# Batch 0 of a linear-attention and mixture-of-experts kernel rearranged: split loads of v, gate weights by GpSimd's queue, copies on either engine, a new written-out order

## The chip, the cores and the metric

The kernel runs on one core of one Trainium2 chip. A core has TensorE (matrix products and transposes, results in PSUM), VectorE and ScalarE (element-wise work; both read PSUM), GpSimd (here it fills constants and issues the loads of the expert weights), SyncE (issues most loads and stores) and 16 DMA engines that move data between the chip's memory (HBM) and the on-core memory (SBUF). Every engine takes its instructions in the order in which the program gives them. They run beside each other and meet at semaphores.

The metric is the device time of one execution in microseconds (us). A trace of one further execution says what each engine did and when.

## The reference, cut to what matters

```python
# q, k, v: batch 8, heads 8, sequence 576, head size 64
phi = lambda x: np.where(x > 0, x, np.exp(x) - 1.0) + 1.0
kv  = einsum('bhsd,bhse->bhde', phi(k), v);  z = phi(k).sum(axis=2)
x   = einsum('bhsd,bhde->bhse', phi(q), kv) / (einsum('bhsd,bhd->bhs', phi(q), z) + 1e-6)
# x as 8 batches of 576 rows of 512; 8 experts, hidden size 1024
logits = x @ w_gate                     # 512 x 8
local  = sigmoid(x @ w_local)           # 512 x 1
# along the rows of a batch: e = argmax(logits) where local < 0.5 or at row 0,
#                            else the expert of the row before
out[b, s] = softmax(logits[b, s])[e] * (relu(x[b, s] @ w1[e]) @ w2[e])
```

So the attention of a batch comes first, then a choice of expert for each row, then two matrix products with that expert's weights.

## The kernel before, in words

The kernel bets that all rows of a batch go to one expert, the one of its row 0. It computes each batch with that expert and counts the rows for which the bet failed; at the end a branch runs `general`, a slow and complete version, if the count is not zero. With these inputs it is zero.

A batch has two groups of four heads, so there are 16 groups, n = 0 to 15; batch a has groups 2a and 2a + 1. One group of q, k or v is 576 KB. All the work is cut into named steps, and `ORDER` (lines 23 to 71) writes out in which order they are issued. That text fixes the order on each engine, and `name/3` says which of four PSUM slots (two banks each) the step uses. The steps:

- `Lk.n`, `Lq.n`, `Lv.n`: loads of a group, by SyncE's queue. k has four buffers, q two, v three; a load waits until the buffer's last reader is done, and everything behind it on SyncE waits as well. Batch 0's q is loaded without its first of nine column blocks; that block comes on its own, in 64 KB pieces, by ScalarE's and by GpSimd's queue (`load_q0`).
- `E0`, `P0`: phi of that first block. `E.x.n`: exp, on ScalarE. `E2.x.n`: relu in place, on ScalarE. `P.x.n`: phi put together on VectorE, min(exp, 1) + relu. For k of batch 0 the relu is replaced by a clamp on VectorE, `CL.n` = max(x + 1, 1), and `P.k` takes the minimum.
- `VC.n`: v copied beside a column of ones. `K.n`: 72 matmuls for kv and z in one, `KC.n` its copy out of PSUM.
- `QL.a`, `Q.n`: transposes of phi(q) on TensorE (last 64 rows; the other 512), `QLC`, `QC` their copies on ScalarE.
- `NL.a`, `N.a.j.h`: numerator and denominator for the last rows, and for half h of group j; `DL`, `D`: the divisions on VectorE. `XL`, `X`: transposes of the result x, with the copies `XLC`, `XC`. `R.a.0`, `R.a.1`: logits of the last rows (row 0 is among them) and of the others, `RC` the copies.
- `PK.a`: the index of row 0's expert. `W.a.0`, `W.a.1`: GpSimd reads the index and issues the loads of w1 and w2, cast from float32 to bfloat16. Three slots keep the experts of earlier batches; a batch whose expert is there loads nothing. `CW`: the copy from slot to working buffer (for batch 0 the other way), on VectorE.
- `H.a.m`: one of eight hidden blocks, `HC` its relu out of PSUM, on ScalarE. `O0.a`, `O.a.i`: output blocks, `OC` the scaled copy, on ScalarE. `ST`: the stores. `S1`, `S2`, `S3`: the softmax factor.
- `HOLD`: a tiny SyncE transfer out of w1's last column, so that the loads behind it wait until batch 0's w1 is there.

Batches overlap: while batch a is in its hidden and output steps, the attention steps of batch a + 1 and the loads for a + 2 run in between. Before batch 0's first useful matmul TensorE runs filler matmuls on zeros (line 705).

Of the kernel before, what the change touches and what calls it, by code (L numbers as in the profile page):

```python
# [951 lines left out]
```

## Time and profile before

| | us |
|---|---|
| three runs, median | 222.1 (222.0 to 224.09) |
| the profiled execution, its own time | 222.04 |
| its span (first to last instruction) | 219.9 |
| busy: TensorE matmuls | 205.6 (94%) |
| busy: ScalarE | 153.3 (70%) |
| busy: VectorE | 151.7 (69%) |
| busy: GpSimd | 12.3 (6%) |

Busy time of TensorE includes the filler matmuls at the start. The rows that the text below shows are of three kinds. A window row gives a stretch of the span, its length, and the busy time of each engine in it, with the number of its instructions. A timeline row gives start, duration, engine, source line, operation, `out<-in` by the program's names, shapes, `xN` for N merged instructions and, in brackets, how long the engine had stood idle and what ended that. A DMA row gives the size and the time from issue to landing. PE is TensorE, PEld its weight loads, DVE VectorE, ACT ScalarE, POOL GpSimd, SPq and ACTq the queues of SyncE and ScalarE.

### The profile page before, as it was taken

To read this page: it belongs to the slowest core of one execution; us is meant where nothing else is said; L and a number is where in the kernel's file an instruction comes from. 1 tells how busy PE (TensorE), PEld (TensorE's weight loads), DVE (VectorE), ACT (ScalarE), POOL (GpSimd) and SP (SyncE) were. 2 spreads that over 40 slices of the span, in tenths; PEclk is the share of its full clock that TensorE was granted. 3 is DMA by queue.
4 is the path that set the end of the run, shared out by engine and by line. 5 is a ranking of instruction groups with operands and counts; after the bars stand their busy time and mean duration, and the time that the engine had idled before them with its cause. 6 is when DMAs were issued, how large, how long until landed. Compare 5 with 4: busy or idle time off the path is not lost.

```text
span 219.9 us, 8513 instructions
## 1 busy us (share of the span) xinstructions
PE 205.6 (94%) x3686; PEld 149.2 (68%) x3701; DVE 151.7 (69%) x428; ACT 153.3 (70%) x226; POOL 12.3 (6%) x41
## 2 busy tenths in 40 slices
PE   7777699999999999999999999999999999999990
PEld 2366578568876877865888668875888577657650
DVE  0687892999889899995795947967957659334000
ACT  3887968798988898899479647898544255327640
POOL 4005000000000011010000000110000001100000
PEclk9999999999999999999999999999999999999998
DMA  5999999387699568999299365999470025990083
GB/s 187 386 345 369 197 215 397 131 286 262 221 271 364 177 266 262 220 212 228 82 298 402 121 218 132 395 189 199 133 289 3 3 101 130 182 189 2 7 332 104
DMA packets 24141, 46.77 MB, mean 213 GB/s; under 512 B 2834, under 2 KB 8978, under 8 KB 23202
## 3 DMA queue, kind: packets, MB, share of 16 engines
q1 hardware_dynamic: 16834, 37.51, 48.2%
q0 software_dynamic: 6832, 8.45, 23.5%
q8 instruction: 31, 0.51, 0.9%
q10 hardware_dynamic: 432, 0.20, 0.4%
q14 instruction: 12, 0.10, 0.1%
HBM read 61.88 MB, written 9.44 MB: 324 GB/s over the span
## 4 chain that ended last, share of the span: by engine, by line
PE 87%; DMA 4%; ACT 3%; issue 1%; DVE 1%; SPq 1%
PE hps L532 29%; PE yps L551 25%; PE nps L349 8%; PE kvps L297 7%; PE tq L308 6%; DMA qraw<-in_q_dram 4%; PE yps L555 4%; PE tx L383 3%; PE lps L416 1%; SPq L138 1%; ACT qT L314 1%; DVE xb L337 1%; PE tql L322 1%; PE npl L368 1%; PE lps L410 1%
## 5 line engine op out<-in xcount | busy, mean ns | idle before, releaser
L532 PE MATMUL hps<-xT,w1cur 128*128 128x288 bf16 x512 | 66.9, 286 | 0.4 <-issue 0.3
L551 PE MATMUL yps<-w2cur,hT 128*128 128x512 bf16 x241 | 58.4, 379 | 0.8
L539 ACT ACTIVATE hT<-hps 128x576 bf16<-128x576 f32 x64 | 41.5, 655 | 24.8 <-PE hps L532 24.7
L532 PEld LDWEIGHTS <-w1cur 128*128 128x128 bf16 x512 | 48.7, 98 | 13.2 <-issue 0.8
L551 PEld LDWEIGHTS <-hT 128*128 128x128 bf16 x256 | 24.1, 98 | 25.5 <-ACT hT L539 0.2
L565 ACT ACTIVATE yo<-yps,pr 128x512 f32<-128x512 f32 x32 | 21.3, 686 | 12.9 <-PE yps L551 10.0
L276 DVE SCALAR_TENSOR_TENSOR fq<-fq,qraw 128x576 f32<-128x576 f32 (+1 forms) x32 | 22.5, 742 | 2.5 <-ACT qraw L247 2.4
L337 DVE TENSOR_TENSOR xb<-nps,rec 128x512 bf16<-128x512 f32 x32 | 22.1, 692 | 1.1
L349 PE MATMUL nps<-kv,qT 64*64 64x65 f32 x1024 | 21.0, 222 | 1.5 <-ACT qT L314 1.0
L297 PE MATMUL kvps<-vone,kraw 64*64 64x65 f32 x1152 | 20.0, 220 | 1.6 <-ACT qT L328 0.8
L314 ACT COPY qT<-tq 128x512 f32<-128x512 f32 x32 | 18.3, 641 | 4.4 <-PE tq L308 4.4
L349 PEld LDWEIGHTS nps<-kv,qT 64*64 64x64 f32 x1024 | 17.5, 134 | 5.4 <-issue 2.4
L297 PEld LDWEIGHTS kvps<-vone,kraw 64*64 64x64 f32 x1152 | 18.2, 134 | 3.5 <-ACT qT L328 1.0
L241 ACT ACTIVATE ek<-kraw 128x1152 f32<-128x1152 f32 x16 | 18.5, 1160 | 2.6 <-DMA kraw<-in_k_dram 2.2
L241 ACT ACTIVATE fq<-qraw 128x1152 f32<-128x1152 f32 (+1 forms) x16 | 18.5, 1156 | 0.7 <-DMA qraw<-in_q_dram 0.7
L269 DVE SCALAR_TENSOR_TENSOR kraw<-ek,kraw 128x1152 f32<-128x1152 f32 x14 | 18.8, 1348 | 0.3 <-ACT kraw L247 0.3
L247 ACT ACTIVATE qraw<-qraw 128x1152 f32<-128x1152 f32 (+1 forms) x16 | 18.3, 1148 | 0.1
L308 PE MATMUL tq<-ident,fq 128*128 128x128 f32 x128 | 16.4, 274 | 0.0
L247 ACT ACTIVATE kraw<-kraw 128x1152 f32<-128x1152 f32 x14 | 16.3, 1166 | 0.0
L308 PEld LDWEIGHTS tq<-ident,fq 128*128 128x128 f32 x128 | 14.3, 141 | 0.5
L388 DVE COPY xT<-tx 128x1024 bf16<-128x1024 bf16 x16 | 10.8, 683 | 3.5 <-PE tx L383 3.5
L288 DVE COPY vone<-vraw 128x1152 f32<-128x1152 f32 x15 | 11.7, 784 | 0.0
(93 smaller groups left out, 176.4 us busy)
## 6 DMA issues: line engine op xcount, KB each, us to landing
kraw<-in_k_dram SPq DMA_DIRECT2D x16, 576.0 KB, 4.9
vraw<-in_v_dram SPq DMA_DIRECT2D x16, 576.0 KB, 6.7
qraw<-in_q_dram SPq DMA_DIRECT2D x14, 576.0 KB, 5.8
w1s<-in_moe_w_dram POOLq DMA_DIRECT2D x7, 1024.0 KB, 10.3
w2s<-in_moe_w_dram POOLq DMA_DIRECT2D x7, 1024.0 KB, 11.5
out_dram<-yo SPq DMA_DIRECT2D x14, 512.0 KB, 5.0
qraw<-in_q_dram SPq DMA_DIRECT2D x2, 512.0 KB, 8.2
w1cur<-in_moe_w_dram POOLq DMA_DIRECT2D x2, 512.0 KB, 7.4
```

The source lines that it names most:

```text
L241: nc.scalar.activation(e[:, :, c0:c1, :], raw_, Act.Exp)
L247: nc.scalar.activation(raw_, raw_, Act.Relu)
L276: nc.vector.scalar_tensor_tensor(e[:, g], e[:, g], 1.0, r[:, g], Alu.min, Alu.add)
L297: nc.tensor.matmul(ps[g * PH:(g + 1) * PH, t, :W], lhsT=f[h, g, c, :], rhs=vo[h, g, c, :], start=(c == 0), stop=(c == C - 1))
L308: nc.tensor.transpose(ps[:, r, i * P:(i + 1) * P], ex_[n, "q"][:, 1 + i + (NC - 1) * r, :, :], identity=ident)
L314: nc.scalar.copy(qT[n][:, :, :SM].rearrange("q t (i p r) -> q r t i p", i=NC - 1, r=2)[:, r], ps[:, r, :].rearrange("q (i t p) -> q t i p" ...
L337: nc.vector.tensor_tensor(dst, ps[:, :, :, :Dh].rearrange("p g (i t) e -> p g i t e", t=2), rec.rearrange("p g (i t o) -> p g i t o", t=2, ...
L349: nc.tensor.matmul(ps[o * PH:(o + 1) * PH, g, (il * 2 + t) * W:(il * 2 + t + 1) * W], lhsT=qT[n][g * PH:(g + 1) * PH, t, i * P + o * PH:i ...
L532: nc.tensor.matmul(ps[:, u, :HS], lhsT=w1b[:, kk, m * P:(m + 1) * P], rhs=xT[b][:, kk, u * HS:(u + 1) * HS], start=(kk == 0), stop=(kk == ...
L539: nc.scalar.activation(hT[b][:, m, :].rearrange("p (u s) -> p u s", u=2), open_.pop(("H", b, m))[:, :, :HS], Act.Relu)
L551: nc.tensor.matmul(ps, lhsT=hT[b][:, m, i * P:(i + 1) * P], rhs=w2b[:, m, :], start=(m == 0), stop=(m == FK - 1))
L565: nc.scalar.activation(ym[:, i, :], ps, Act.Copy, scale=pr[:, i:i + 1])
```

## The change

Eight things change together.

1. v of groups 0 and 1 is loaded, copied beside its ones and used in two pieces, of five and of four column blocks (`Lv.n`, `Lv.n.1`; the same for `VC` and `K`).
2. `CL.1` writes into k's third buffer instead of in place (`CL.0` keeps v's third buffer).
3. The gate weights (w_gate, w_local) come by GpSimd's queue at the very start, as four rows of 4 KB and four of 512 B in k's fourth buffer. Nine TensorE transposes (`WT`) and a copy on VectorE (`WG`) turn them into the layout needed. Before, SyncE loaded them in rows of 32 and 4 bytes. The iota and its cast on GpSimd go.
4. The first column block of batch 0's q is one load by ScalarE's queue.
5. w1 of batch 0 comes in three pieces (first quarter, second quarter, second half) instead of two halves. There are two `HOLD`s now: one on the second quarter, one, much later in the order, on the end.
6. Batch 0's expert index is taken straight from PSUM, ahead of the copy of the logits.
7. Copies may run on either engine: a `^` behind a step in `ORDER` puts it on the engine other than its usual one. 23 of 64 `HC`, 20 of 40 `OC`, 14 `E2` and 2 `QC` so move from ScalarE to VectorE; 11 `VC` (three of them pieces of batch 0), 9 `XC`, 8 `KC` and 5 `XLC` are on ScalarE.
8. The filler is nine small matmuls and 15 large ones ahead of `WT`, instead of 19 large ones ahead of `QL.0`. `ORDER` is new as a whole, with new PSUM slots. The steps of the branch at the end (`FR`) stand at other places.

```diff
@@ ORDER (the first words; the old ones are in the listing above)
+Lq.0 Lk.1 FILL/0 Lv.1 Lv.1.1 Lv.0 Lk.0 Lq.1 Lv.0.1 E0.0 P0.0 E.k.1 CL.1 WT/1 E.q.0 P.k.1 QL.0/2 VC.1^
+E2.q.0^ QLC.0 K.1/3 VC.1.1^ P.q.0.0 K.1.1 E.k.0 P.q.0 CL.0 Q.0/2 Lq.2 VC.0^ Lk.3 P.k.0 E.q.1 Lk.2 KC.1^
+VC.0.1 QC.0 K.0/3 E2.q.1^ K.0.1 P.q.1.0 KC.0^ P.q.1 E.q.2 NL.0/2 N.0.0.1/3 DL.0 Lq.3 E.k.3 Lv.3 WG D.0.0.1
+XL.0/2 Lv.2 Q.1/1 XLC.0^ R.0.0/2 QC.1 N.0.0.0/3 RC.0.0 D.0.0.0 W.0.0 E.k.2 N.0.1.1/2 N.0.1.0/1 PK.0 E2.k.3
+D.0.1.1 E.q.3 D.0.1.0 BK.0 P.k.3 VC.3^ W.0.1 X.0.0/3 X.0.1/2 XC.0.0 XC.0.1^ K.3/1 E2.q.2^ E2.q.3^ R.0.1/3
+HOLD.0 H.0.0/2 P.q.3 Lk.5 H.0.1/0 HC.0.0 P.q.2 H.0.2/2 HC.0.1 H.0.3/0 KC.3 RC.0.1 S1.0 QL.1/1 CW.0.0 Q.3/3
+QLC.1 HC.0.2 H.0.4/1 E2.k.2 HC.0.3^ H.0.5/2 QC.3 P.k.2 Q.2/0 HC.0.4^ H.0.6/3 QC.2 VC.2 N.1.1.1/1 HC.0.5 Lv.5
...
-    fills = {("QL", 0): 19}
+    fills = {("WT",): 15}
...
-        def load_q0(n):
-            load(q0[:, n], q, n, 0, 1, nc.scalar if n else nc.gpsimd)
+        def load_q0():
+            run = C * Dh
+            nc.scalar.dma_start(out=q0.rearrange("p j g d -> p (j g) d"),
+                                in_=bass.AP(q.tensor, 0, [[run, P], [P * run, 2 * NJ], [1, Dh]]))
+
+        CV = (0, (C + 1) // 2, C)
...
+        wgf = kraw[NKR - 1].rearrange("p g c d -> p (g c d)")[:DK]
+        nc.gpsimd.dma_start(out=wgf[:, :P * E], in_=moe_w_gate.rearrange("(ko ki) e -> ko (ki e)", ki=P))
+        nc.gpsimd.dma_start(out=wgf[:, P * E:], in_=moe_w_local.rearrange("(ko ki) e -> ko (ki e)", ki=P))
...
         def relus(n, x, c0=0, c1=C):
             raw_ = slot(n, x)[:, :, c0:c1, :]
-            nc.scalar.activation(raw_, raw_, Act.Relu)
+            if on_act("E2", x, n, act=True):
+                nc.scalar.activation(raw_, raw_, Act.Relu)
+            else:
+                if c1 - c0 == C:
+                    raw_ = raw_.rearrange("p g c d -> p (g c d)")
+                nc.vector.tensor_scalar(raw_, raw_, 0.0, None, Alu.max)
...
-            return (vraw[2] if n == 0 else kraw[n]).rearrange("p g c d -> p (g c d)")
+            return (kraw[2] if n else vraw[2]).rearrange("p g c d -> p (g c d)")
...
+        def on_act(*name, act=False):
+            return (name in other) != act
+
+        def copy(dst, src, *name, act=False):
+            (nc.scalar.copy if on_act(*name, act=act) else nc.vector.tensor_copy)(dst, src)
...
+        def gate_turn():
+            ps = bank("wgp", "WT")
+            for e in range(E + 1):
+                nc.tensor.transpose(ps[:, e * DK:(e + 1) * DK],
+                                    wgf[:, e:P * E:E] if e < E else wgf[:, P * E:],
+                                    identity=ident[:DK, :DK])
...
+            if b == 0 and cs[0] == NC - 1:
+                top(b, lps[0:1, NC - 1, :E])
             nc.vector.tensor_copy(lt_all[:, b, cs[0]:cs[-1] + 1], lps[:, cs[0]:cs[-1] + 1])
...
+        FP = (0, F // 4, F // 2, F)
...
-                for h in range(2):
-                    nc.gpsimd.dma_start(out=wcur[0][:, :, h * F // 2:(h + 1) * F // 2],
-                                        in_=src[:, :, h * F // 2:(h + 1) * F // 2])
+                for f0, f1 in zip(FP, FP[1:]):
+                    nc.gpsimd.dma_start(out=wcur[0][:, :, f0:f1], in_=src[:, :, f0:f1])
...
+            if on_act("HC", b, m, act=True):
+                nc.scalar.activation(dst, src, Act.Relu)
+            else:
+                nc.vector.tensor_scalar(dst, src, 0.0, None, Alu.max)
...
+            if on_act("OC", b, i, act=True):
+                nc.scalar.activation(dst, src, Act.Copy, scale=pr[:, i:i + 1])
             else:
-                nc.scalar.activation(yl, ps[:, :D // 2], Act.Copy, scale=pr[:, i:i + 1])
+                nc.vector.tensor_scalar(dst, src, pr[:, i:i + 1], None, Alu.mult)
...
+            for _ in range(9):
+                nc.tensor.matmul(fill[:32, :32], lhsT=zero[:, :32], rhs=zero[:, :32], start=True, stop=True)
```

More of the change, by code (lines that the diff above doesn't have):

```diff
@@ L482, in weights, with hold @@
                     in_=src, cond=wl[b][2] > 0)
-        def hold():
-            nc.sync.dma_start(out=there, in_=wcur[0][0:1, 0, F - 1:F])
+        def hold(i):
+            src = wcur[1][0:1, 0, D - 1:D] if i == 2 else wcur[0][0:1, 0, (i + 1) * F // 2 - 1:(i + 1) * F // 2]
+            nc.sync.dma_start(out=there[:, i:i + 1], in_=src)
         def use(b, x):
@@ L679 @@
         ENG = {"PE": ET.PE, "ACT": ET.Activation, "DVE": ET.DVE, "POOL": ET.Pool, "SP": ET.SP}
-        after = {"DVE": ("FI",), "POOL": ("FI",), "SP": ("ST", B - 1, 2), "ACT": ("OC", B - 1, 2),
-                 "PE": ("O", B - 1, NC - 1)}
-        for e, d in after.items():
+        for e in ENG:
             op(("FR", e), lambda e=e: load_flag(ENG[e]))
@@ L697 @@
                 got[name] = int(at)
+            if word.endswith("^"):
+                other.add(name)
         assert sorted(map(str, order)) == sorted(map(str, run))
```

195 lines of the change are left out of this document (96 added, 99 removed).

## The prediction, written before the result

> **What bounds the kernel now.** I read the page first, for the engines' shares, and then cut the span where TensorE's work changes its nature: at the first useful matmul, at the first hidden-layer matmul of batch 0 (H.0.0) and at the last matmul.
>
> ```profile
> span 219.9 us, 8513 instructions
> PE 205.6 (94%) x3686; PEld 149.2 (68%) x3701; DVE 151.7 (69%) x428; ACT 153.3 (70%) x226; POOL 12.3 (6%) x41
> ```
>
> ```profile
> 0.00:9.36 9.36, 7.08 (x20) 2.54 (x20) 2.63 (x8) 4.67 (x6) 2.30 (x17) 1.00 0.77 268
> 9.36:26.76 17.40, 11.94 (x420) 9.96 (x421) 15.00 (x36) 15.28 (x19) 2.83 (x3) 1.00 1.10 316
> 26.76:214.62 187.86, 186.62 (x3253) 136.73 (x3264) 134.06 (x385) 132.93 (x202) 7.21 (x21) 1.00 0.71 204
> 51.72:81.91 30.19, 29.90 (x709) 23.14 (x710) 27.55 (x71) 27.58 (x39) 1.16 (x5) 1.00 0.76 266
> 108.24:133.83 25.59, 25.45 (x504) 19.28 (x501) 19.02 (x57) 17.98 (x27) 0.27 (x3) 1.00 0.70 241
> 214.62:219.90 5.28, 0.00 (x0) 0.00 (x0) 0.00 (x0) 0.48 (x1) 0.00 (x0) 0.89 0.31 94
> ```
>
> Each row is a stretch: its bounds, its length, then the busy time of TensorE's matmuls, its weight loads, VectorE, ScalarE and GpSimd. From 26.76 to 214.62 TensorE idles 187.86 - 186.62 = 1.24 us. That stretch is TensorE's own work, and the change leaves it the same matmuls. So the change can win three things: a useful start before 9.36, the 17.40 - 11.94 = 5.46 us idle ahead of H.0.0, and the 1.24. I therefore follow H.0.0. The profiled execution's own time is 222.04 us, its span and 2.14 around it; the median of the three runs is 222.1.
>
> time = start of H.0.0 + 187.86 + 5.28 + 2.14.
>
> **Arrivals.** Loads of 576 KB (512 KB for batch 0's q) come in one behind another.
>
> ```profile
> 5.22 1.16 ACT L241 ACTIVATE ek<-kraw 128x1152 f32<-128x1152 f32 x1 [2.18 <-DMA kraw<-in_k_dram]
> 7.12 0.76 DVE L261 TENSOR_SCALAR vraw<-kraw 128x1152 f32<-128x1152 f32 x1 [5.58 <-DMA kraw<-in_k_dram]
> 7.35 0.42 ACT L250 ACTIVATE fq<-q 128x256 f32<-128x256 f32 x1 [0.97 <-DMA q<-in_q_dram]
> 12.84 1.06 ACT L241 ACTIVATE fq<-qraw 128x1024 f32<-128x1024 f32 x1 [0.55 <-DMA qraw<-in_q_dram]
> ```
>
> The second load is in at 7.12, the sixth at 12.84: 2176 KB in 5.72 us, 1.5 us per 576 KB. In the new order k1 is second (7.1), the pieces of v1 come at 7.9 and 8.6, v0's first at 9.4, k0 at 10.9, q1 at 12.3, v0's second at 12.9. Batch 0's first q columns (128 KB) now go by ScalarE's queue alone.
>
> ```profile
> q<-in_q_dram ACTq DMA_DIRECT2D x1, 64.0 KB, 4.4
> out_dram<-yo SPq DMA_DIRECT2D x2, 256.0 KB, 2.8
> w1cur<-in_moe_w_dram POOLq DMA_DIRECT2D x2, 512.0 KB, 7.4
> w1s<-in_moe_w_dram POOLq DMA_DIRECT2D x7, 1024.0 KB, 10.3
> ```
>
> Half of that took 4.4 us, issued at 1.0, so the whole lies between 5.4 and 1.0 + 8.8 = 9.8. I take 7.1: GpSimd's half is in at 7.35 today, and ScalarE's next work needs k1, at 7.1, in any case.
>
> **VectorE up to the k-v product of group 0.**
>
> ```profile
> 7.79 0.76 DVE L261 TENSOR_SCALAR kraw<-kraw 128x1152 f32<-128x1152 f32 x1
> 8.46 0.29 DVE L253 TENSOR_SCALAR q<-q 128x256 f32<-128x256 f32 x1
> 9.12 1.35 DVE L271 TENSOR_TENSOR kraw<-vraw,ek 128x1152 f32<-128x1152 f32 x1
> 10.39 1.35 DVE L271 TENSOR_TENSOR kraw<-kraw,ek 128x1152 f32<-128x1152 f32 x1
> 12.33 1.29 DVE L276 SCALAR_TENSOR_TENSOR fq<-fq,qraw 128x512 f32<-128x512 f32 x2
> 13.53 0.58 DVE L302 COPY kv<-kvps 128x130 f32<-128x130 f32 x2
> ```
>
> Start to start, VectorE pays 0.67 for a clamp (7.12 to 7.79), 0.66 for P0 (8.46 to 9.12), 1.27 for P.k and 1.20 for the two parts of P.q. E2.q.0, a relu that moves here from ScalarE, is not in the trace on this engine; its nearest row is the clamp of 1152 columns, so 0.60 for 1024, and ScalarE's 1.06 for as many columns (the row at 12.84) is the other end. E0 ends at 7.5. Then P0 0.66, CL.1 0.67, P.k.1 1.27, E2.q.0 0.60, P.q.0 1.20 (ends 11.9), CL.0 0.67, P.k.0 1.35: the end is 13.9. It used to be P.k.1 that came last, 10.39 + 1.35 = 11.74, with the copy of v1 behind it. The split of v hides behind VectorE; clamping k into free slots takes nothing out of this sum.
>
> **From there to the choice of the expert.**
>
> ```profile
> 13.97 0.65 PE L368 MATMUL npl<-kv,qT 64*64 64x65 f32 x16 [0.21 <-ACT fq L241]
> 15.97 1.11 ACT L314 COPY qT<-tq 128x512 f32<-128x512 f32 x2
> 16.10 0.28 DVE L399 COPY xT<-txl 128x256 bf16<-128x256 bf16 x1
> 16.44 0.30 PE L410 MATMUL lps<-wg,xT 128*64 128x9 bf16 x8 [0.60 <-DVE xT L399]
> 17.37 0.15 DVE L427 FIND_INDEX8 i<-m,lt_all 1x8 uint32<-1x8 f32 x1
> 18.77 1.94 POOL L475 DMA_DIRECT2D w1cur<-in_moe_w_dram  x2 [15.14 <-DVE den L334]
> 25.14 1.28 PE L297 MATMUL kvps<-vone,kraw 64*64 64x65 f32 x72 [0.17 <-PE tx L383]
> ```
>
> K.0 (1.28) runs from 14.0 to 15.3, KC.0 adds 0.29, NL.0 starts at 15.7 instead of 13.97. From NL.0 to XLC took 16.10 - 13.97 = 2.13, so XLC.0 has its input at 17.8. But XLC.0 moves to ScalarE, behind E.k.3, and here the change adds a wait. On SyncE's queue Lq.2 now stands ahead of Lk.3 and Lk.2, and waits for P.q.0 (11.9); before, Lk.3 went out ahead of all of batch 1's loads and waited for nothing. A lone 576 KB load takes 2.8 us (the 256 KB store) plus 320 KB at the pace, 0.83: 3.65.
>
> ```profile
> 0.99 0.95 SPq L138 DMA_DIRECT2D kraw<-in_k_dram  x2
> 28.73 0.75 SPq L486 DMA_DIRECT2D there<-w1cur  x1
> 35.22 0.18 POOL L468 COPY seen<-w2cur 1x1 bf16<-1x1 bf16 x1 [13.62 <-DMA w2cur<-in_moe_w_dram]
> ```
>
> The first load of all, 5.22 - 0.99 = 4.2, is the other end. So q2 is in at 15.6, k3 at 17.1, and E.k.3 (1.16) runs to 18.3. XLC.0 lies between VectorE's 0.28 and 0.55, ScalarE's price for twice the columns; with 0.45 it ends at 18.7. R.0.0 starts at 18.8 instead of 16.44, 2.4 later. Queued behind XLC.0 on ScalarE is QC.1.
>
> From R.0.0 to the index it was 17.52 - 16.44 = 1.08; the maximum read straight from PSUM leaves out the copy ahead of it, 0.2: 19.7. GpSimd issued 18.77 - 17.52 = 1.25 later: 20.9. The first half of w1 landed 7.4 behind its issue (26.2), the second half let SyncE go at 28.73, so a half costs 2.55 and the new first quarter is 7.4 - 1.3 = 6.1 behind its issue. By w1 of later batches, 10.3 for two halves, it is 5.2 + 1.3 = 6.5; by the 256 KB store, 2.8 + 1.3 = 4.1. I take 5.5, nearest to the same transfer today but with fewer loads beside it: 26.4. The gate weights' loads leave SyncE's queue, and their nine small transposes fit into TensorE's idle time before QL.0: nothing on the path.
>
> **The other way to H.0.0, by group 1.**
>
> ```profile
> 21.60 0.17 DVE L334 TENSOR_SCALAR den<-nps 128x8 f32<-128x8 f32 x1 [0.15 <-PE nps L349]
> 22.65 0.15 DVE L334 TENSOR_SCALAR den<-nps 128x8 f32<-128x8 f32 x1
> 23.68 1.35 DVE L269 SCALAR_TENSOR_TENSOR kraw<-ek,kraw 128x1152 f32<-128x1152 f32 x1
> 26.74 3.79 PEld L532 LDWEIGHTS <-w1cur 128*128 128x128 bf16 x32
> 39.75 0.38 PE L551 MATMUL yps<-w2cur,hT 128*128 128x512 bf16 x1
> ```
>
> A division is 22.65 - 21.60 = 1.05. QC.1 (1.11) runs from 18.7 to 19.8. N.0.0.0 follows R.0.0 (72 small matmuls take 1.28, its 32 take 0.57) and its division ends at 20.8; 0.3 for the tag, and the two divisions of group 1 end at 22.2 and 23.2. P.k.3 (1.35) ends at 24.6. From the end of P.k.3, 23.68 + 1.35 = 25.03, to H.0.0 it was 1.7 (K.3 and R.0.1), so H.0.0 can start at 26.3. Both ways meet at 26.4, against 26.76 before: what group 0 loses at the start the order regains, since N.0.0.1 and Q.1 now run while XLC.0 waits.
>
> The sum is 26.4 + 187.86 + 5.28 + 2.14 = 221.7. Behind H.0.0 the copies change engines under TensorE's cover; rival three has the price if that cover goes. The last copy, now on VectorE, differs by under 0.1.
>
> **Rivals.** A change under 1% (2.2 us) I count as none.
>
> *One, the start comes free.* If XLC.0 and QC.1 wait for nothing, VectorE's own list remains. From 7.5 it is the 0.66 + 0.67 + 1.27 + 0.60 + 1.20 + 0.67 + 1.27 of above, 0.3 + 0.6 + 1.2 (v0's second piece, group 1's relu and phi), five divisions (5 x 1.05, the last columns' rather less), 0.6 for the index, the copy and the tag, and P.k.3's 1.35: 15.6, so 23.1. With the 1.7, H.0.0 starts at 24.8: 220.1; with half of the 1.24 gone as well, 219.5. For it: the tiny rows of the gate weights no longer sit in the stream of loads. Against it: Lk.3 behind Lq.2.
>
> *Two, slower: w2 comes too late.* It was in at 35.22, and its first user ran at 39.75. Its request is now 20.9 - 18.77 = 2.1 later, plus one more issue, 0.97: 38.3, for a use at 39.4. It costs from 39.4 on, and over 1% from 42.0 on. GpSimd issues it about 23.8 (three issues behind 20.9), while VectorE runs P.k.3, the relus of q2 and q3 (0.67 each) and then P.q.3 and P.q.2 (1.20 each), 5.1 in all. If it can't issue meanwhile, w2 lands at 43.4, a stall of 4.0: 225.7. One pair of rows speaks for it:
>
> ```profile
> 19.55 1.17 POOL L475 DMA_DIRECT2D w1cur<-in_moe_w_dram  x1
> 19.66 0.75 DVE L288 COPY vone<-vraw 128x1152 f32<-128x1152 f32 x1
> ```
>
> The second issue took 1.17 beside VectorE's copy, the first (1.94 - 1.17) 0.77: 0.4 more, about half of the copy. At half, the 5.1 add 2.6: 40.9, a stall of 1.5, 223.2, which is not yet 1%. [...]
>
> *Three, slower: VectorE fills up behind H.0.0.*
>
> ```profile
> L337 DVE TENSOR_TENSOR xb<-nps,rec 128x512 bf16<-128x512 f32 x32 | 22.1, 692 | 1.1
> ```
>
> Between H.3.0 and H.4.0 (the row from 108.24) it now gets two hidden copies (0.76 each, from 0.29 for 130 and 0.69 for 512 columns out of PSUM), a q copy of two 0.69, a relu 0.67 and an output copy 0.69, in all 4.3, and gives away two kv copies and XLC, 0.9 (and an XC, which I leave out). The order also puts one more K, Q and N into this stretch: 1.35 + 1.2 + 1.05 + 0.3 = 3.9 for VectorE, 1.28 + 0.57 and a transposition for TensorE. That is 19.02 + 3.4 + 3.9 = 26.3 of at least 27.4 us, at most 96%. In the row from 51.72 it was 27.55 of 30.19, 91%, and TensorE idled 0.29, so it should hold. It decides from 4% dearer copies on; at 15% the list needs 30.2, 2.8 us over: 224.5.
>
> *Four, slower: the first q columns take until 9.8,* and everything starts 2.7 later: 224.4.
>
> **Numbers.** Forecast 221.7: 0.70. Rival one 0.15, of which 0.12 lies beyond 1%; two 0.05, three 0.07, four 0.03. The forecast's own range is 221.2 to 223.2, by the first quarter of w1 (6.5: +1.0), the relu at ScalarE's price (+0.5) and the late load (+0.55). The range for 8 in 10 takes in most of rival one and the nearer half of the slower ones: 219.5 to 224.3. Faster 0.12, same 0.73, slower 0.15.
>
> **What would show it.** R.0.0 near 18.8, with E.k.3 starting on the landing of k3, shows the added wait; H.0.0 between 26.0 and 27.2 shows the balance; 187 to 188.5 us from H.0.0 to the last matmul show the cover. I am wrong if H.0.0 starts before 25.2 or after 28, if TensorE waits for w2 at the first output matmul, or if it idles more than 3 us behind H.0.0 with VectorE as the releaser.

## The result, and the profile after

The changed kernel takes 221.39 us (median of 16 executions, 219.28 to 223.98) against 222.58 us (16 executions, 221.47 to 225.4) of the kernel before, run side by side: a ratio of 0.9932, 95% interval 0.9904 to 0.9959. So it is faster by 0.7%, which is less than the 1% that was set as the limit of "no change". The forecast of 221.7 is 0.3 away.

The total is right, but not the parts. Here are three lines of the changed kernel's page: the span, the busy times, and the granted clock in 40 slices of 5.5 us.

```profile
span 220.6 us, 8567 instructions
...
PE 207.2 (94%) x3702; PEld 152.7 (69%) x3715; DVE 177.8 (81%) x459; ACT 131.2 (59%) x197; POOL 13.6 (6%) x41
...
PEclk9978879999999999999999999999999999999997
```

VectorE went from 69% to 81%, ScalarE from 70% to 59%: that is the exchanged copies. The profiled execution's own time is 222.17, somewhat above the median. The clock line has a dip in slices 3 to 6 that the kernel before doesn't have; in the trace's clock record these are three windows at half speed, 9.97 to 13.39, 20.21 to 23.63 and 27.04 to 30.45 us, each 3.41 us long.

The windows view of the changed kernel, cut at the same places (H.0.0 starts at 28.74, the last matmul ends at 215.12):

```profile
0.00:9.36 9.36, 7.50 (x35) 3.51 (x35) 2.91 (x7) 4.11 (x6) 2.40 (x16) 1.00 0.79 262
9.36:28.74 19.38, 14.11 (x418) 12.45 (x419) 15.74 (x37) 14.45 (x21) 3.21 (x4) 0.78 0.96 274
28.74:215.12 186.38, 185.59 (x3255) 136.78 (x3265) 158.62 (x416) 112.66 (x171) 7.96 (x21) 1.00 0.74 206
215.12:220.60 5.48, 0.01 (x2) 0.00 (x0) 0.48 (x1) 0.00 (x0) 0.00 (x0) 0.78 0.30 96
```

H.0.0 comes 1.98 later than in the kernel before (26.76), and from there to the last matmul it is 1.48 shorter (187.86). The idle time of TensorE in it fell from 1.24 to 0.79; its busy time fell by 1.0 as well, with the same matmuls. With the measured terms the sum of the forecast reads 28.74 + 186.38 + 5.48 + 1.57 = 222.17, the profiled execution.

Where the start lost: ScalarE, TensorE, VectorE and GpSimd in the timeline of the changed kernel, one fence each.

```profile
17.07 1.17 ACT L241 ACTIVATE fq<-qraw 128x1152 f32<-128x1152 f32 x1 [1.23 <-DMA qraw<-in_q_dram]
18.58 1.16 ACT L241 ACTIVATE ek<-kraw 128x1152 f32<-128x1152 f32 x1 [0.34 <-DMA kraw<-in_k_dram]
19.65 0.35 ACT L292 COPY xT<-txl 128x256 bf16<-128x256 bf16 x1
```

```profile
9.94 2.23 PE L306 MATMUL kvps<-vone,kraw 64*64 64x65 f32 x72 [0.99 <-ACT vone L292]
...
20.06 0.31 PE L427 MATMUL lps<-wg,xT 128*64 128x9 bf16 x8 [1.42 <-ACT xT L292]
...
26.53 1.83 PE L306 MATMUL kvps<-vone,kraw 64*64 64x65 f32 x72 [0.62 <-DVE kraw L274]
28.29 0.59 PE L433 MATMUL lps<-wg,xT 128*128 128x9 bf16 x16
28.74 1.60 PE L556 MATMUL hps<-xT,w1cur 128*128 128x288 bf16 x6
```

```profile
24.92 1.35 DVE L274 SCALAR_TENSOR_TENSOR kraw<-ek,kraw 128x1152 f32<-128x1152 f32 x1
```

```profile
22.11 2.32 POOL L499 DMA_DIRECT2D w1cur<-in_moe_w_dram  x3 [18.35 <-DVE rec L344]
24.40 0.92 POOL L501 DMA_DIRECT2D w2cur<-in_moe_w_dram  x1
39.29 0.18 POOL L492 COPY seen<-w2cur 1x1 bf16<-1x1 bf16 x1 [13.97 <-DMA w2cur<-in_moe_w_dram]
```

XLC.0 stands at 19.65 behind E.q.2 (17.07) and E.k.3 (18.58), both of which waited for a load; R.0.0 starts when it is done, at 20.06. K.1 and K.3 take 2.23 and 1.83 us where the clock is halved; at full clock K.1 with its two pieces takes 1.54 (e1 and e10 below) and K.3 1.28. H.0.0 waits for nothing: it runs right behind R.0.1 (28.29), which runs behind K.3, and K.3 waited for P.k.3 (24.92). The first quarter of w1 had landed 0.3 us earlier, at 28.44.

### The profile page after: what moved, and what is told of

The parts are those of the page before. It is cut to its first block, busy times and chain, and to the rows that moved or that the text cites. A ratio compares the mean times of both kernels' runs of the same rounds, so it can differ in the third digit from the quotient of the medians.

```text
span 220.6 us, 8567 instructions
## 1 busy us (share of the span) xinstructions
PE 207.2 (94%) x3702; PEld 152.7 (69%) x3715; DVE 177.8 (81%) x459; ACT 131.2 (59%) x197; POOL 13.6 (6%) x41
## 4 chain that ended last, share of the span: by engine, by line
PE 87%; DMA 5%; DVE 2%; ACT 2%; issue 1%; SPq 0%; DVEq 0%; ACTq 0%
PE hps L556 29%; PE yps L578 25%; PE kvps L306 9%; PE nps L357 7%; PE tq L317 6%; DMA kraw<-in_k_dram 5%; PE yps L582 4%; PE tx L391 3%; PE lps L433 2%; ACT ek L241 1%; PE npl L376 1%; PE lps L427 1%; PE tql L330 1%; DVE xb L345 1%; DVE kraw L274 1%
## 5 line engine op out<-in xcount | busy, mean ns | idle before, releaser
L565 ACT ACTIVATE hT<-hps 128x576 bf16<-128x576 f32 x41 | 26.7, 657 | 37.7 <-PE hps L556 28.8
L306 PE MATMUL kvps<-vone,kraw 64*64 64x65 f32 x1152 | 21.8, 229 | 2.0 <-ACT vone L292 1.0
L306 PEld LDWEIGHTS kvps<-vone,kraw 64*64 64x64 f32 x1152 | 19.7, 143 | 3.6 <-ACT vone L292 1.5
L274 DVE SCALAR_TENSOR_TENSOR kraw<-ek,kraw 128x1152 f32<-128x1152 f32 x14 | 18.8, 1346 | 2.1 <-ACT kraw L248 2.1
L567 DVE TENSOR_SCALAR hT<-hps 128x576 bf16<-128x576 f32 x23 | 17.1, 752 | 4.2 <-PE hps L556 4.0
L241 ACT ACTIVATE ek<-kraw 128x1152 f32<-128x1152 f32 x16 | 18.8, 1173 | 2.3 <-DMA kraw<-in_k_dram 2.3
L593 ACT ACTIVATE yo<-yps,pr 128x512 f32<-128x512 f32 x16 | 11.0, 690 | 11.3 <-PE yps L578 11.2
L317 PE MATMUL tq<-ident,fq 128*128 128x128 f32 x128 | 17.3, 280 | 0.0
L292 ACT COPY qT<-tq 128x512 f32<-128x512 f32 x28 | 15.9, 644 | 0.7 <-PE tq L317 0.6
L292 ACT COPY xT<-tx 128x1024 bf16<-128x1024 bf16 x9 | 9.1, 1014 | 10.7 <-PE tx L391 10.7
L595 DVE TENSOR_SCALAR yo<-yps,pr 128x512 f32<-128x512 f32 x16 | 11.7, 744 | 2.0 <-PE yps L578 1.9
L248 ACT ACTIVATE kraw<-kraw 128x1152 f32<-128x1152 f32 x10 | 11.7, 1169 | 0.0
```

The lines of the kernel that those rows point to most:

```text
L241: nc.scalar.activation(e[:, :, c0:c1, :], raw_, Act.Exp)
L274: nc.vector.scalar_tensor_tensor(r, e, 1.0, r, Alu.min, Alu.add)
L292: (nc.scalar.copy if on_act(*name, act=act) else nc.vector.tensor_copy)(dst, src)
L306: nc.tensor.matmul(ps[g * PH:(g + 1) * PH, t, :W], lhsT=f[h, g, c, :], rhs=vo[h, g, c, :], start=(c == 0), stop=(c == C - 1))
L317: nc.tensor.transpose(ps[:, r, i * P:(i + 1) * P], ex_[n, "q"][:, 1 + i + (NC - 1) * r, :, :], identity=ident)
L565: nc.scalar.activation(dst, src, Act.Relu)
```

## The experiments

Every run was timed against the kernel before on the same chip. "Tail" is the stretch from H.0.0 to the end of the last matmul in the profiled execution.

### Who wins: the start or the tail (e4, e3)

The two halves of the change were put together crosswise. e4 keeps the changed kernel up to H.0.0 and takes the old order behind it, without exchanged copies:

```diff
-... R.0.1/3 HOLD.0 H.0.0/2 P.q.3 Lk.5 H.0.1/0 HC.0.0 P.q.2 H.0.2/2 HC.0.1 ...   (the changed order)
+... R.0.1/0 HOLD.0 H.0.0/3 E2.k.2 P.q.2 H.0.1/1 HC.0.0 RC.0.1 P.q.3 H.0.2/3 ... (the old order, no ^)
```

> The other way round: the changed kernel up to H.0.0, then the order of the kernel before, with every copy on its usual engine. Theory A: H.0.0 starts at 28.5 to 29.0, the stretch behind it is 187.5 to 188.5, and the ratio to the kernel before is 1.004 to 1.011. Rival, the start is what wins: the ratio is 0.990 to 0.996, as with the whole change.

Measured: 223.1 us, ratio 1.0005 (0.9965 to 1.0046). H.0.0 at 27.76.

```profile
27.76:215.59 187.83, 187.34 (x3262) 136.75 (x3262) 133.71 (x385) 132.46 (x201) 7.11 (x21) 1.00 0.71 205
```

The old tail takes its old time (187.83), and with it the gain is gone. So the gain of 0.7% sits behind H.0.0. The start is worth nothing by the ratio, between the two theories: its loss shows in H.0.0, but less than in the profile of the whole change. Four profiles have this same work ahead of H.0.0 (the change itself, e4, e9, and e6 with other fillers at its very start): H.0.0 lies at 28.74, 27.76, 27.19 and 27.73 in them. The change's own profile is the latest of the four. In e4 alone H.0.0 waits for w1:

```profile
27.76 2.50 PE L558 MATMUL hps<-xT,w1cur 128*128 128x288 bf16 x19 [0.47 <-DMA w1cur<-in_moe_w_dram]
```

Part of the gain lies outside the span from first to last instruction. An execution's time is longer than its span (recorded to 0.1 us) by 1.93 to 2.25 us in the kernel before (81 executions), by 1.50 to 1.68 in the changed one (16), by 1.88 to 1.99 in e4, and by 1.50 to 1.70 in e3 and e5, which have the old start and the changed tail. So about 0.5 of the 1.2 us gained comes with the tail in this way. What that time consists of is not shown.

e3 is the reverse, the old start and the changed tail:

```diff
-... R.0.1/0 H.0.0/3 ...                     (the kernel before)
+... R.0.1/3 HOLD.0 H.0.0/2 P.q.3 Lk.5 ...   (from here the changed order and copies)
```

> The kernel before up to H.0.0 (its loads, gate weights, halves of w1 and order), then the changed kernel's order and its exchanged copies. Theory A, the change loses about 2 us ahead of H.0.0 and wins about 1.5 behind it: H.0.0 starts at 26.5 to 27.0, from there to the last matmul it is 186.2 to 186.8 instead of 187.86, and the ratio to the kernel before is 0.986 to 0.992, better than the changed kernel's 0.993. Rival, what is won lies in the rearranged start (the loads, the weights in three pieces, the state in which it leaves group 1): the stretch behind H.0.0 is 187.5 to 188.5 and the ratio 0.998 to 1.003.

Measured: 232.35 us, ratio 1.0394 (1.0335 to 1.0454). Neither theory said so. The waits of TensorE behind H.0.0 in e3 (us in total, times, the longest), and two rows of its timeline:

```profile
PE nps L363 <- issue: 5.9, 4, 2.6
PE kvps L312 <- issue: 2.3, 3, 1.3
```

```profile
75.53 0.99 PE L363 MATMUL nps<-kv,qT 64*64 64x65 f32 x52
...
79.17 0.39 PE L363 MATMUL nps<-kv,qT 64*64 64x65 f32 x11 [2.65 <-issue]
```

"issue" means that TensorE waited for nothing that the profile shows. It stopped in the middle of a run of 64 like matmuls. The queues of the page name a transfer that belongs to no step of the kernel:

```profile
q8 instruction: 31, 0.51, 0.9%
```

31 packets of 16 KB. By the name of the queue I take them for the program's own code. In the trace each of the six stops lies at a multiple of 256 recorded TensorE instructions from the next (a few records are missing), and ends 1.3 to 1.6 us after one of these packets has arrived:

| stop (us) | length | recorded instruction | distance | code packet ended | restart behind it |
|---|---|---|---|---|---|
| 43.59 | 0.74 | 1474 | | 42.83 | 1.50 |
| 57.15 | 0.84 | 1986 | 512 | 56.41 | 1.58 |
| 76.52 | 2.65 | 2753 | 767 | 77.80 | 1.37 |
| 98.08 | 1.07 | 3521 | 768 | 97.72 | 1.43 |
| 125.80 | 1.33 | 4546 | 1025 | 125.81 | 1.33 |
| 141.52 | 1.45 | 5058 | 512 | 141.57 | 1.40 |

That made a third theory, C, read from these distances: TensorE's code comes in blocks of 256 instructions; where a block is late, TensorE stands still; and so the time hangs on where the borders of the blocks fall in the order. The trace of the kernel before fits it: its longest "issue" stop is 0.43 us and ends at 18.13, and counted from there in steps of 256 recorded instructions, exactly one 16 KB packet ends between any two neighbouring borders, 28 in all.

### Moving nothing but the borders (e5, e12, e6)

e5 is e3 with 14 tiny fillers (32 columns, 28 instructions, 27 ns apart) at the start, where TensorE has nothing to do. The borders then fall where they do in the changed kernel.

```diff
+            for _ in range(14):
+                nc.tensor.matmul(fill[:32, :32], lhsT=zero[:, :32], rhs=zero[:, :32], start=True, stop=True)
```

> Run e3 with 14 tiny filler matmuls (28 TensorE instructions) at the very start; nothing else. In e3's trace TensorE stopped six times behind H.0.0 with nothing that it waited for (0.74, 0.84, 2.65, 1.07, 1.33, 1.45 us, 8.1 in all), at its instructions 1474, 1986, 2753, 3521, 4546 and 5058 as recorded: the distances are 512, 767, 768, 1025 and 512, multiples of 256. Theory C, TensorE's code comes in blocks of 256 instructions and a block that is late stops it, so what counts is where the borders of the blocks fall: with 28 instructions more they fall where they do in the changed kernel (944 ahead of H.0.0 in place of 916), which has no such stop; the six stops are gone, the stretch behind H.0.0 is 185.5 to 187.5 instead of 197.6, and the ratio to the kernel before is 0.983 to 0.993 instead of 1.039. Rival, the order of the changed kernel does not fit the loads that the other start leaves behind: the stops and the ratio stay within 0.01 of e3's.

Measured: 222.44 us, ratio 0.9978 (0.9948 to 1.0008): 10 us less than e3. Of the six stops one is left (0.96 us, at recorded instruction 1473, 1.49 behind its packet; the profile puts it down to VectorE). So e3's loss against the kernel before was the borders. The ratio is not quite what was expected: this start reached H.0.0 only at 28.35, with another border stop of 1.30 ahead of it, and the tail took 187.64, just above the expected 187.5.

e12 does the reverse to the kernel before: half a block more ahead of everything, nothing else.

```diff
-    fills = {("QL", 0): 19}
+    fills = {("QL", 0): 15}
+            for _ in range(68):
+                nc.tensor.matmul(fill[:32, :32], lhsT=zero[:, :32], rhs=zero[:, :32], start=True, stop=True)
```

> The kernel before with 68 tiny and 15 large fillers at the start in place of 19 large ones: 128 TensorE instructions more ahead of everything, half a code block, at about the same time; nothing else. Theory C: the kernel before has no stop over 0.5 us behind H.0.0 where its borders fall now; with the borders moved by half a block some blocks are late, two to six stops of 0.4 to 2 us at recorded instructions that lie a multiple of 256 apart, ratio 1.005 to 1.03. Rival, the stops belong to the changed order alone: no stop, ratio 0.997 to 1.003.

Measured: 247.14 us, ratio 1.1045 (1.0983 to 1.1106), far more than expected. TensorE's waits behind H.0.0 and its longest stop:

```profile
PE npl L368 <- issue: 5.9, 2, 3.7
PE tql L322 <- issue: 2.5, 1, 2.5
PE nps L349 <- issue: 0.7, 1, 0.7
```

```profile
163.67 0.39 PE L368 MATMUL npl<-kv,qT 64*64 64x65 f32 x11
167.78 0.48 PE L368 MATMUL npl<-kv,qT 64*64 64x65 f32 x5 [3.72 <-issue]
```

The border before this stop was passed at 161.93; the packet started 3.56 us later, at 165.48, and ended at 166.38. I read that as a wait among the loads and stores, which no run tested: from 158 to 167 the windows view gives the 16 DMA engines a busy share of 1.03. H.0.0 slipped to 33.84 (two border stops, of 2.96 and 1.30, lie ahead of it) and the tail to 206.92 (five, 9.7 together). That is 14 of the some 25 us; eight windows at half clock came with them, and how the rest divides between the clock and work pushed into busier stretches was not tried.

e6 puts 40 instructions more ahead of the changed kernel (22 tiny fillers more, two large ones fewer), which leaves everything else.

```diff
-    fills = {("WT",): 15}
+    fills = {("WT",): 13}
-            for _ in range(9):
+            for _ in range(31):
```

> The changed kernel with 22 tiny filler matmuls more and two large ones fewer at the very start, so 40 TensorE instructions more ahead of everything, as many as e1 had ahead of H.0.0; the work in the idle stretches of batch 0 is untouched. Theory C (borders of code blocks): two stops of 0.9 to 1.5 us behind H.0.0, near 67 and 86 us, as in e1, and a ratio of 1.000 to 1.006 instead of 0.993. Rival, e1 was slow because its fillers stood in the way: no stop, ratio 0.990 to 0.996.

Measured: 222.56 us, ratio 0.9988 (0.9951 to 1.0025). TensorE's waits behind H.0.0:

```profile
PE tq L317 <- issue: 1.4, 1, 1.4
PE txl L402 <- DVE xb L345: 1.1, 1, 1.1
```

One of the two stops expected came, at 66.81; the other, at 128.78, is an ordinary wait for VectorE (its packet had landed, and its place is no border). The point of the ratio is back at the kernel before (the two intervals still touch, from 0.9951 to 0.9959), with nothing done but 40 instructions that take next to no time.

### The exchanged copies (e9)

```diff
-... HC.0.3^ H.0.5/2 QC.3 P.k.2 Q.2/0 HC.0.4^ ... OC.7.4^ ...
+... HC.0.3 H.0.5/2 QC.3 P.k.2 Q.2/0 HC.0.4 ... OC.7.4 ...    (every ^ behind H.0.0 taken out)
```

> The changed kernel, with every copy, relu and cast behind H.0.0 back on its usual engine (all the ^ behind H.0.0 taken out); order, PSUM slots and TensorE's instructions are the changed kernel's. The tail of the changed kernel takes 185.4 to 185.6 us without cold stretches and stops of TensorE, the tail of the kernel before 187.4. Theory: the tail wins by its order of TensorE's work, and the exchanged engines only cover it; then without them TensorE waits for ScalarE's copies in places, 1 to 4 us more idle behind H.0.0, ratio 0.996 to 1.010. Rival, the exchange matters nothing: the stretch is 185.4 to 186.6 and the ratio 0.990 to 0.996.

Measured: 230.42 us, ratio 1.0354 (1.0311 to 1.0397); the tail and TensorE's largest waits in it:

```profile
27.19:223.76 196.57, 188.41 (x3255) 136.95 (x3265) 134.71 (x386) 132.46 (x202) 7.69 (x21) 1.00 0.70 196
```

```profile
PE nps L359 <- issue: 2.8, 2, 1.6
PE kvps L308 <- issue: 0.9, 1, 0.9
PE tx L393 <- ACT hT L567: 0.7, 1, 0.7
PE hps L558 <- DVE kv L294: 0.5, 1, 0.5
```

The direction was expected, the size (9 us more than with the exchange, 230.42 for 221.39) was not. The whole list of waits in the tail comes to 6.7 us. Besides waits for copies, 3.6 us of it are border stops, though the borders lie at the same instructions as in the changed kernel; that the packets meet other loads when the times shift is a reading that was not tested. The rest of the loss was not taken apart. So the changed order needs the exchange. The exchange in the old order was not tried.

### The clock (e1, e7, e11)

e1 puts 20 large fillers into the idle stretches of batch 0:

```diff
-    fills = {("WT",): 15}
+    fills = {("WT",): 15, ("K", 1): 4, ("K", 0): 1, ("NL", 0): 1, ("XL", 0): 2, ("R", 0, 0): 5, ("X", 0, 1): 5,
+             ("K", 3): 2}
```

> The changed kernel with 20 more filler matmuls of 512 columns on zeros, put where TensorE stood idle in batch 0 (4 before K.1, 1 before K.0, 1 before NL.0, 2 before XL.0, 5 before R.0.0, 5 before X.0.1, 2 before K.3); nothing else. In the changed kernel's profile the clock was 0.5 in three windows of 3.4 us (9.97 to 13.39, 20.21 to 23.63, 27.04 to 30.45). Theory B, the clock costs it: if the idle stretches are what takes the clock down, it stays at 1.0 from 10 to 31 us, K.1 takes 1.28 again instead of 2.23, the first hidden blocks run at full speed, H.0.0 starts at 27.3 to 28.2 instead of 28.7, the mean granted clock is 0.99 or more, and the ratio to the kernel before is 0.983 to 0.988 (after: 0.993). Rival, the clock costs nothing because the weights' landing and VectorE set H.0.0: the clock is full and the ratio stays 0.991 to 0.995. Second rival, the clock does not follow the idle time: the three windows stay at 0.5.

Measured: 223.79 us, ratio 1.001 (0.9971 to 1.005). The clock did what theory B says: no window at half speed between 7 and 219 us. K.1 took 1.54, not 1.28, and H.0.0 came at 28.47, later than expected. But the 40 instructions moved the borders. Behind H.0.0:

```profile
PE tq L318 <- issue: 1.4, 1, 1.4
PE hps L557 <- issue: 0.9, 1, 0.9
PE hps L557 <- DVE w1cur L519: 0.6, 1, 0.6
```

e7 repeats it with exactly 256 instructions more, so that the borders behind H.0.0 stay, and with fillers moved off the path:

```diff
+    fills = {("WT",): 8, ("K", 1): 4, ("K", 0): 4, ("NL", 0): 1, ("XL", 0): 2, ("R", 0, 0): 5, ("X", 0, 0): 7}
+            for _ in range(121):   # small fillers, 9 before
```

> As e1, the changed kernel with fillers in the idle stretches of batch 0 (4 before K.1, 4 before K.0, 1 before NL.0, 2 before XL.0, 5 before R.0.0, 7 before X.0.0, none before K.3), and at the start 121 tiny and 8 large ones in place of 9 and 15, so that exactly 256 TensorE instructions more stand ahead of H.0.0 and the borders of the code blocks fall where they do in the changed kernel. Theory B and C together: the clock is at 1.0 from 10 to 31 us, no stop behind H.0.0, 185.4 to 186.0 us from H.0.0 to the last matmul, H.0.0 at 27.6 to 28.4, ratio 0.983 to 0.989. Rival, the clock in batch 0 costs nothing that the end sees: ratio 0.991 to 0.995.

Measured: 224.35 us, ratio 1.0063 (1.0031 to 1.0095). The expectation failed in batch 0: one block more had to come in there, among batch 0's loads, and TensorE stopped for it 2.33 us at 17.89.

```profile
PE fill L744 <- issue: 2.8, 3, 2.3
```

R.0.0 moved to 24.30 and H.0.0 to 31.93. Of the 4.2 us at R.0.0, 1.1 were there before the stop, since k of group 0 landed later; the rest is the stop and a window at half speed behind it (19.89 to 23.30). Behind H.0.0 the tail is 186.40 with one stop of 0.46.

e11 changes no count at all: the nine tiny fillers become nine large ones in the idle stretches.

```diff
-    fills = {("WT",): 15}
+    fills = {("WT",): 15, ("K", 1): 4, ("R", 0, 0): 3, ("X", 0, 0): 2}      (and the nine small ones go)
```

> The changed kernel with the nine tiny fillers of the start replaced by nine large ones in the idle stretches (4 before K.1, 3 before R.0.0, 2 before X.0.0): the same number of TensorE instructions ahead of H.0.0, so the code blocks' borders stay behind H.0.0. Theory B: at most one cold window between 10 and 31 us in place of three, K.1 in 1.28 us instead of 2.23, the first hidden block at full clock (0.8 us), no stop behind H.0.0, ratio 0.986 to 0.990 instead of 0.993. Rival, the clock's windows do not follow the idle stretches, or their cost is hidden by loads: ratio 0.991 to 0.996.

Measured: 221.62 us, ratio 0.9919 (0.9884 to 0.9954). The mean granted clock of its executions has a median of 0.991, the changed kernel's 0.982; the ratio can't be told from 0.9932. Its profiled execution, at 224.26 us the longest of the twelve, still has two windows at half speed in a row, 26.34 to 33.17, so nine fillers at these places do not keep the clock up every time. So what the clock costs was not settled by a ratio. Two other numbers size it. Between the start of H.0.0 and its relu it is 2.00 us in the changed kernel, where a cold window covers it, and 1.17 in e1: 0.83 for one window. And of 81 executions of the kernel before, 38 had a mean clock of 0.994 or more and a median of 222.1 us, 22 one of 0.979 to 0.985 and 223.1: 1.0 us for 0.013 of the clock.

### The start (e2, e8), and a version from all of it (e10)

e2 sends Lk.3 out ahead of Lq.2:

```diff
-... WT/1 E.q.0 P.k.1 ... Q.0/2 Lq.2 VC.0^ Lk.3 P.k.0 ...
+... WT/1 Lk.3 E.q.0 P.k.1 ... Q.0/2 Lq.2 VC.0^ P.k.0 ...
```

> The changed kernel with one load moved: Lk.3 goes out on SyncE's queue right behind batch 0's loads, ahead of Lq.2, which waits for P.q.0. Theory A, the wait that the change put ahead of Lk.3 delays E.k.3, with it XLC.0 and the choice of the expert: E.k.3 starts before 15.5 instead of at 18.58, XLC.0 at 18.0 to 18.5 instead of 19.65 (it then waits for the transposes of x), the index comes 1.2 to 1.6 earlier, H.0.0 starts at 27.1 to 27.7 instead of 28.7, and the ratio is 0.986 to 0.989. Rival, group 1's chain on VectorE (P.k.3, two divisions) or the clock sets H.0.0 as well: R.0.0 is earlier, H.0.0 stays within 0.4 of 28.7, and the ratio stays at 0.992 to 0.994.

Measured: 222.46 us, ratio 0.9929 (0.9888 to 0.9971), no change. k3 was in at 14.95, yet ScalarE's rows read:

```profile
17.51 1.16 ACT L243 ACTIVATE fq<-qraw 128x1152 f32<-128x1152 f32 x1 [0.60 <-DMA qraw<-in_q_dram]
18.58 1.15 ACT L243 ACTIVATE ek<-kraw 128x1152 f32<-128x1152 f32 x1
19.63 0.35 ACT L294 COPY xT<-txl 128x256 bf16<-128x256 bf16 x1
```

E.q.2 also stands ahead of XLC.0 on ScalarE, and it waits for Lq.2. The wait on SyncE was not the one that came last. e8 is e2 with E.q.2 behind QC.1:

```diff
-... P.q.1 E.q.2 NL.0/2 ... E.k.3 ... XLC.0^ R.0.0/2 QC.1 N.0.0.0/3 ... PK.0 E2.k.3 ...
+... P.q.1 NL.0/2 ... E.k.3 ... XLC.0^ R.0.0/2 QC.1 E2.k.3 E.q.2 N.0.0.0/3 ... PK.0 ...
```

> As e2 (Lk.3 ahead of Lq.2 on SyncE), and on ScalarE E.q.2 moved from ahead of E.k.3 and XLC.0 to behind QC.1, with E2.k.3 right behind QC.1; TensorE's order is untouched. In e2 k3 was in at 14.95 and XLC.0 still ran at 19.63, because E.q.2, which waits for q2 (17.42), stood ahead of E.k.3 and XLC.0 on ScalarE. Theory A with ScalarE's queue in the place of SyncE's: XLC.0 at 17.5 to 18.0, R.0.0 at 18.6 to 18.9 instead of 20.06 (behind Q.1), the index 1.2 to 1.5 earlier, H.0.0 at 26.6 to 27.6 instead of 28.7, and the ratio 0.984 to 0.990. Rival, the weights' landing moves less than their request because the loads that share the engines set it: R.0.0 is earlier, H.0.0 stays above 28.0, ratio 0.991 to 0.995.

Measured: 220.11 us, ratio 0.9871 (0.9818 to 0.9924). In its profile the clock was halved from 11 to 18 us, so the transposes came late and XLC.0 only at 18.98; H.0.0 is at 28.06, no stop follows, and the tail is

```profile
28.06:213.44 185.38, 184.59 (x3255) 136.10 (x3264) 158.87 (x416) 112.70 (x171) 8.00 (x21) 1.00 0.74 208
```

The point of the ratio is where it was expected, the steps were later than expected, and the interval overlaps the changed kernel's.

e10 adds nine large fillers for the nine tiny ones, and VC.3 ahead of E.q.3, for which K.3 waited in e8:

```diff
-    fills = {("WT",): 15}
+    fills = {("WT",): 15, ("K", 1): 4, ("K", 0): 2, ("X", 0, 0): 3}
-... PK.0 D.0.1.1 E.q.3 D.0.1.0 BK.0 P.k.3 VC.3^ ...
+... PK.0 D.0.1.1 VC.3^ E.q.3 D.0.1.0 BK.0 P.k.3 ...
```

> As e8 (Lk.3 early, E.q.2 behind QC.1), with VC.3 ahead of E.q.3 on ScalarE (K.3 waited 1.1 us for it in e8), and the nine tiny fillers of the start replaced by nine large ones in the idle stretches (4 before K.1, 2 before K.0, 3 before X.0.0), so that TensorE's instruction count ahead of H.0.0 and the borders of its code blocks stay. Theories A, B and C together: clock at 1.0 through most of batch 0, K.3 0.6 to 0.8 earlier, H.0.0 at 26.7 to 27.6 (e8: 28.06), no stop behind it, 185.3 to 185.7 from there to the last matmul, ratio 0.980 to 0.986 (e8: 0.987). Rival, w1's landing sets H.0.0 near 27.5 to 28 whatever stands ahead: ratio 0.986 to 0.990.

Measured: 219.66 us, ratio 0.9868 (0.9834 to 0.9902). Its windows, and its clock:

```profile
9.36:26.58 17.22, 12.48 (x425) 9.84 (x425) 15.75 (x37) 14.70 (x22) 3.20 (x4) 1.00 1.04 306
26.58:211.87 185.29, 184.53 (x3255) 136.12 (x3264) 158.92 (x416) 112.75 (x171) 7.99 (x21) 1.00 0.74 208
```

```profile
PEclk9999999999999999999999999999999999999998
```

H.0.0 is at 26.58, before even the kernel before, the clock is full, and no stop follows. It is faster than the kernel before by 1.3%; its interval ends where the changed kernel's begins. That it did not beat e8 by the ratio, in spite of the clock, fits the small price of the clock above, though 6 and 12 executions don't separate half a per cent.

## Why the prediction was right in the total and wrong in its parts

**The start.** The arrivals were well placed: k1 at 7.16 (7.1 predicted), the end of P.k.0 at 13.85 (13.9), NL.0 at 15.90 (15.7), E2.q.0 on VectorE 0.72 from start to start (0.60). The first q columns came at 5.36, at the early bound. The first step that failed is the lone load: Lq.2 was priced at 3.65, with 4.2 as the other end, and took 5.3 (issued at 11.67, landed at 16.99). It was not alone: v0's second piece, ahead of it, landed at 13.24. The added wait was named, and R.0.0 did start on it, but at 20.06 in place of 18.8; and e2 and e8 show that it reached XLC.0 through E.q.2 on ScalarE's queue as much as through Lk.3 on SyncE's, while the prediction had named Lk.3 alone.

"Both ways meet at 26.4" is then the step that was wrong. In the profile, H.0.0 is 2.3 later, and the way by group 1 set it: P.k.3 ended at 26.27 in place of 24.6, 1.7 late, and from there to H.0.0 it took 2.5 in place of 1.7, with K.3 at half clock. The way by w1 was nearly as late, at 28.44: 1.2 by the later request (22.11 for 20.9) and 0.8 by the first quarter (6.3 for 5.5). In the three other profiles with this start the quarter took 4.7 to 6.0 and H.0.0 came at 27.2 to 27.8: still 0.8 to 1.4 late. Of these e4 waited for w1; in e9 and e6 it had landed 0.9 and 1.2 before H.0.0, and group 1 set the start again. The prediction had set 28 as the point from which it is wrong here, and the profile passed it.

**The cover.** "187.86 unchanged" was wrong the other way. It took the matmuls to cost the same in any order. Without cold windows and stops, the changed tail takes 185.3 to 185.4 (e8, e10), the old one 187.8 (before, e4): 2.5 less, and nearly all of it in TensorE's busy time: 187.34 in e4, 184.53 in e10, with the same matmuls and 0.5 and 0.8 us idle. (The trace of e10 lacks a few matmul records, so its busy time reads somewhat low.) Summed from start to start, passing from one operation to another took 18.0 us in e10 (143 times) against 20.5 in e4 (147), while steps within one operation took the same in both, 167.0 and 167.1. Passing from an output block to a numerator, for one, happened twice and took 0.59 in e10, and seven times and 1.84 in e4. No run tried such passings alone, so this is an account of the gain and not a test. In the changed kernel a cold window at H.0.0 gave 0.8 of it back.

**The sum.** Against the profiled execution the first term was 2.3 too small, the second 1.5 too large, and the last two, 5.28 + 2.14 for a measured 5.48 + 1.57, 0.4 too large together; the median then lies 0.8 below the profiled execution. That 221.7 came within 0.3 of the median is luck: errors of opposite sign cancelled.

**The rivals.** One (the start comes free) did not happen: R.0.0 waited for ScalarE. Two (w2 too late, its issue held up by VectorE): the three issues of w1 took 2.32 together, 0.77 each, and w2's 0.92; w2 was in at 39.29 and first used at 42.12. No block shows in these rows: w2's issue, from 24.92 on beside P.k.3, took no longer than the 0.97 that was allowed for it. That GpSimd stands still for the whole of VectorE's work, which the 225.7 supposed, was shown by no run. Three (VectorE fills up): VectorE is busy 158.62 of 186.38 us, and the list of TensorE's waits behind H.0.0 is empty. The page's groups have the price of the copies that moved to it, 0.75 (0.76 estimated) and 0.74 (0.69):

```profile
L567 DVE TENSOR_SCALAR hT<-hps 128x576 bf16<-128x576 f32 x23 | 17.1, 752 | 4.2 <-PE hps L556 4.0
...
L595 DVE TENSOR_SCALAR yo<-yps,pr 128x512 f32<-128x512 f32 x16 | 11.7, 744 | 2.0 <-PE yps L578 1.9
```

In e9, without the exchange, copies and code hold TensorE up instead. Four (first q columns late) was wrong, they came early.

**What it had not seen at all.** The clock, and the code. It did have the rows for both: PEclk, and q8. Two rows of the kernel before show the sign as well:

```profile
18.13 0.45 PE L349 MATMUL nps<-kv,qT 64*64 64x65 f32 x11 [0.43 <-issue]
...
24.58 0.38 PE L383 MATMUL tx<-identb,xb 128*128 128x128 bf16 x4 [1.17 <-DVE xb L337]
```

These two restarts are 256 recorded instructions apart and lie 1.48 and 1.46 behind the end of a code packet (16.65 and 23.12); the second is put down to VectorE, whose result was there 0.8 before. The five more fillers of part 8 and the nine transposes of part 3, both priced at nothing, shift every border behind them, by 10 and 18 instructions; with a shift of 40 more the gain no longer shows (e6). The chance of "slower" should have held this as a rival, with a price of several per cent.

## What to carry to other kernels

Where TensorE is busy 94% of the span, as here, first look for "issue" stops and whether they are 256 instructions apart: in e3 they were, no wait in the kernel explained them, and 28 instructions more at the start decided over several per cent (1.0394 in e3, 0.9978 in e5). When an edit changes the number of TensorE instructions, compare it with a version padded back to the old borders before its time is put down to its idea. And before a load is moved forward, follow every queue from the step that waits: the in-order engine that uses the data may stand on another load, as ScalarE did in e2, where k3 was in at 14.95 and XLC.0 still ran at 19.63, behind E.q.2.

## What the hardware showed that had not been expected

**Code is fetched late enough to stop TensorE.** Over e3, e5, e7, e9 and e12 the stops at borders lasted 0.3 to 3.7 us and ended 1.3 to 1.6 us after a 16 KB packet. At four stops of e12 the packet had started only 3.9, 2.2, 3.6 and 0.7 us after the previous border was passed, so there the time in which 256 instructions run (2.1 to 5.5 us at the stops of e3 and e12) has to hold this delay, the transfer (0.90 for the packet at 165.48) and the 1.3 to 1.6. In the kernel before the code of 8 of 28 blocks is there with 0.6 us or less to spare (an estimate: border passed, less end of packet, less 1.4). In e12, with the borders moved by half a block, the time was 10% longer (ratio 1.1045), and the stops were 14 of the some 25 us.

**The clock falls without a long gap.** In the changed kernel no idle stretch of TensorE between 9 and 27 us was over 1.42 us, and still two windows there ran at half clock; the kernel before, with gaps up to 1.17, had none in its profile. What took the clock down is not shown. With fillers in the idle stretches it stayed up there in the profiles of e1 and e10; those of e7 and e11 still have windows at half speed (19.89 to 23.30, and 26.34 to 33.17).

**The same start reaches H.0.0 at times 1.5 us apart** (27.19 in e9 to 28.74 in the changed kernel's profile). Of these 1.5, 0.5 is there at R.0.0, 0.4 comes between R.0.0 and the end of P.k.3, and 0.6 from there to H.0.0; in the later profile a window at half speed lies over a part of each of these two last stretches, in e9 the one window ends at 19.64, just behind the start of R.0.0. The first quarter of w1 took 4.7 to 6.3 us over the four profiles, but only e4 waited for it.
